# Exponentials and sines grouped by table set with two argument buffers in an SSM table, and one shared reciprocal for the attention denominators

## The chip, the cores and the metric

The kernel runs on one core of a Trainium2 chip. The metric is the device time of one execution in microseconds (us).

The engines are TensorE (PE in the profile, its weight loads PEld), VectorE (DVE), ScalarE (ACT), GpSimd (POOL) and SyncE (SP), which here only issues DMAs. Each engine works through its own stream of instructions.

## The reference, cut to what matters

Two independent computations share the input sizes and are written side by side in the output: linear attention with a softmax feature map (columns 0 to 447), and a diagonal state-space model as an FFT convolution (columns 448 to 895).

```python
# A: S = 2048, D = 448, 16 heads of 28
phi_q = concatenate([softmax(pq), softmax(-pq)], axis=-1)      # likewise phi_k
kv  = einsum("bhsf,bhsd->bhfd", phi_k, v)
z   = einsum("bhsf->bhf", phi_k)
num = einsum("bhqf,bhfd->bhqd", phi_q, kv)
den = einsum("bhqf,bhf->bhq", phi_q, z)[..., None] + 1e-6      # one value per head and row
o   = num / den
a   = o.transpose(...).reshape(B, S, D) @ wo

# B: D = 448 channels, N = 256 states, L = 2048
logdA = dt * (A_re + 1j * A_im);  dB = dt * (B_re + 1j * B_im)
P = exp(logdA[:, :, None] * l[None, None, :])
K = einsum("dn,dnl,dn->dl", C, P, dB).real                     # the table K
y = irfft(rfft(u) * rfft(K))[:L] + u * Dskip                   # per channel
```

## The kernel before: the parts that matter

The core works through four stages in turn: the attention; the coefficients of the SSM; the table K; the FFT convolution. The change touches the end of the attention and the table K.

*Attention denominators.* A denominator belongs to a head, not to each of its 28 columns. The kernel computed it for all columns: ZBBD holds the sums z repeated over each head's columns, and in each of 16 groups (4 column chunks dc, 4 row quarters sc) the denominators come out as a full tile, to be inverted in float32.

```python
for dc in range(4):
    for sc in range(4):
        # num_ps += KVBD.T @ PHIQ over 2 signs and 2 or 3 chunks   (L396)
        # den_ps += ZBBD.T @ PHIQ, as many matmuls again           (L408)
        nc.vector.tensor_scalar_add(den[plo:phi, :], dps[plo:phi, :], 1e-6)      # L417
        nc.vector.reciprocal(rden[plo:phi, :], den[plo:phi, :])                  # L419
        nc.vector.tensor_tensor(out=ot[...], in0=nps[...], in1=rden[...], op=ALU.mult)
```

*The table K.* A power exp(l·logdA) with l = 64·hi + lo is a product of a factor in hi (32 values) and one in lo (65 values). The factors in hi are built by a doubling recurrence on VectorE (UR, UI). Those in lo come from TensorE and ScalarE: a matmul of 4 rows makes their arguments (args), ScalarE takes Exp, cosine (Sin with a bias) and Sin of them, and VectorE multiplies. TensorE then contracts over the 128 states of a half. There are 2 halves of the states (nch) with 9 blocks of 48 slots and one of 16 each; a slot is one channel.

```python
for nch in range(2):
    # powers of the step, P[1] .. P[16] ("P tables"): VectorE
    for sb in range(0, NDQ, SBQ):                        # 10 blocks
        # 4 DMAs of coefblk; 10 small copies on GpSimd
        for k in (1, 2, 4, 8, 16):                       # recurrence: 6 VectorE operations a level, L628 to L633
            ...
        with tc.tile_pool(name=f"k_psarg{blk_idx}", bufs=1, space=PSUM) as psa_pool:
            for bq in range(0, nq, BQ):                  # 2 chunks of 24 slots
                args = psa_pool.tile([128, 8 * 512], F32, name="args", tag="args")    # 4096 columns; kps takes the same space
                for bs in range(nd):
                    nc.tensor.matmul(args[:, base:base + N_ARG], lhsT=coef[0:4, slot, :], rhs=R[0:4, :], ...)
                nc.scalar.activation(E[...],  argview(0),    ACT.Exp)                  # L661
                nc.scalar.activation(CL[...], argview(N_LO), ACT.Sin, bias=bias_hp)    # L662
                nc.scalar.activation(SL[...], argview(N_LO), ACT.Sin)                  # L664
                # WR = E * CL, WI = E * SL on VectorE
        with tc.tile_pool(name=f"k_psk{blk_idx}", bufs=1, space=PSUM) as psk_pool:
            # kps: 2 matmuls a slot of UR, UI with WR, WI; then to Ts by ScalarE (first half)
            # or added to Ts by VectorE (second half)
```

The softmax here doesn't subtract the row's maximum and nothing guards it: scores larger than these inputs give would overflow.

## Time and profile before

The median was 1204.45 us of 4 runs (1203.22 to 1206.53) when I predicted; with the runs made beside later ones, 1203.44 of 15. The stages of the profiled run, read from the first start of the instruction that opens each (dt is the first ScalarE operation of the coefficients, args the first matmul of K, the DMAs of the finished table close K):

| stretch | us |
|---|---|
| start to dt (attention) | 320.2 |
| dt to first args (coefficients) | 53.4 |
| first args to the table's DMAs (K) | 411.6 |
| the table's DMAs to the end (FFT) | 416.4 |

Three groups of the page of before say most. Each row has a line and what it does, then busy us and mean ns of one instruction, then the engine's idle time just before them and who ended it.

```profile
L644 PE MATMUL args<-Rconst,coefblk 4*128 4x130 bf16 x896 | 102.9, 308 | 169.6 <-ACT SL L664 126.6
...
L661 ACT ACT_TABLE_LOAD x39 | 50.0, 1283 | 77.8 <-PE args L644 74.6
...
L419 DVE RECIPROCAL rden_sb<-den_sb 128x512 f32<-128x512 f32 (+1 forms) x16 | 53.5, 3346 | 0.0
```

TensorE idles 126.6 us for ScalarE, and ScalarE 74.6 us for TensorE: the two wait for each other. The reciprocal has no idle time before it: there VectorE is the bound.

### The profile page before, as it was taken

How to read it: one execution, taken by the hardware profiler on the slowest of the kernel's cores; microseconds unless marked ns; L12 is line 12 of the kernel's file. 1: busy time of each engine (PE TensorE's matmuls, PEld its weight loads, DVE VectorE, ACT ScalarE, POOL GpSimd, SP SyncE). 2: the span in 40 equal slices, each digit the busy share in tenths (PEclk: the TensorE clock that was granted, in tenths of full speed). 3: DMA queues.
4: the chain of work that ended last, by engine and by line, in shares of the span. 5: the costliest groups of instructions: out<-in, count | busy, mean ns of one | idle time of the engine just before them, and what ended most of it. 6: DMA issues, size and time to landing. Idle time of an engine off the chain costs nothing.

```text
span 1201.6 us, 12236 instructions
## 1 busy us (share of the span) xinstructions
PE 544.9 (45%) x4427; PEld 243.1 (20%) x4427; DVE 639.1 (53%) x1301; ACT 401.4 (33%) x382; POOL 87.9 (7%) x243
## 2 busy tenths in 40 slices
PE   1986534867731333433243333311433345163198
PEld 0221100512111333333233323300100110010021
DVE  2339337569958865684766675439221223832500
ACT  0113320000016577667757576613221222031000
POOL 2000000100004321120211110010000000000000
PEclk9995665669575555555555555555555555555555
DMA  5000000000140000000000000051565557056511
GB/s 124 1 0 1 0 0 0 5 6 1 31 111 18 3 2 3 4 3 4 3 3 5 3 2 4 2 93 46 153 205 144 147 134 242 13 138 185 216 31 31
DMA packets 73636, 63.53 MB, mean 53 GB/s; under 512 B 34984, under 2 KB 68800, under 8 KB 73344
## 3 DMA queue, kind: packets, MB, share of 16 engines
q1 hardware_dynamic: 37866, 35.58, 11.2%
q10 hardware_dynamic: 35710, 27.17, 8.2%
q8 instruction: 35, 0.57, 0.2%
q14 instruction: 25, 0.20, 0.1%
HBM read 30.73 MB, written 28.52 MB: 49 GB/s over the span
## 4 chain that ended last, share of the span: by engine, by line
PE 28%; DVE 25%; DMA 20%; ACT 19%; issue 5%; ACTq 1%; SPq 1%; POOL 0%; DVEq 0%; POOLq 0%
PE args L644 7%; ACT CL L662 4%; DVE rden_sb L419 4%; ACT L662 4%; ACT SL L664 4%; PE ps_qk L195 3%; DMA SD_k<-stgA 3%; PE ops L1006 3%; PE ops L1004 3%; DVE stgA L882 2%; ACT L661 2%; DMA s2k<-SD_k 2%; DMA s2k<-SD_u 2%; DMA SD_u<-stgA 2%; DMA UD<-in_B_u_dram 2%
## 5 line engine op out<-in xcount | busy, mean ns | idle before, releaser
L644 PE MATMUL args<-Rconst,coefblk 4*128 4x130 bf16 x896 | 102.9, 308 | 169.6 <-ACT SL L664 126.6
L644 PEld LDWEIGHTS <-coefblk 4*128 4x128 bf16 x896 | 96.3, 142 | 173.7 <-issue 166.5
L871 PE MATMUL psA<-xin,FA 32*128 32x448 bf16 x128 | 52.1, 563 | 106.0 <-ACT stgA L880 33.4
L687 PE MATMUL kps<-WR,UR 128*32 128x65 bf16 x896 | 36.6, 256 | 127.8 <-ACT SL L664 115.9
L670 DVE TENSOR_TENSOR WR<-E,CL 128x1560 bf16<-128x1560 bf16 (+2 forms) x40 | 36.9, 922 | 105.4 <-ACT CL L662 105.4
L882 DVE CAST stgA<-psA 128x1792 bf16<-128x1792 f32 x16 | 32.4, 2024 | 82.8 <-DMA SD_k<-stgA 24.4
L661 ACT ACT_TABLE_LOAD x39 | 50.0, 1283 | 77.8 <-PE args L644 74.6
L661 ACT ACTIVATE E<-args 128x1560 bf16<-128x1560 f32 (+2 forms) x40 | 55.4, 1385 | 27.7 <-PE args L644 27.5
L439 ACT CAST osb<-ps_out 128x448 bf16<-128x448 f32 x8 | 4.2, 530 | 168.5 <-PE ps_out L430 158.4
L662 ACT ACTIVATE CL<-args,bias_hp 128x1560 bf16<-128x1560 f32 (+2 forms) x40 | 59.0, 1475 | 0.5
L880 ACT CAST stgA<-psA 128x1792 bf16<-128x1792 f32 x16 | 26.4, 1651 | 88.1 <-PE psA L871 28.6
L664 ACT ACTIVATE SL<-args 128x1560 bf16<-128x1560 f32 (+2 forms) x40 | 55.0, 1376 | 0.0
L689 PEld LDWEIGHTS <-UI 128*32 128x32 bf16 x896 | 32.7, 164 | 104.7 <-issue 101.7
L419 DVE RECIPROCAL rden_sb<-den_sb 128x512 f32<-128x512 f32 (+1 forms) x16 | 53.5, 3346 | 0.0
L195 PE MATMUL ps_qk<-xT,Wqkv 128*128 128x512 bf16 (+3 forms) x128 | 39.9, 425 | 28.7 <-DMA xT<-in_A_x_dram 26.6
L902 PE MATMUL xps<-s2k,CB 128*32 128x448 bf16 x256 | 31.6, 567 | 46.1 <-DMA s2k<-SD_u 22.9
L662 ACT ACT_TABLE_LOAD x40 | 51.3, 1283 | 0.2
L1004 PE MATMUL ops<-ZA,IA 128*32 128x448 bf16 x64 | 35.4, 556 | 35.3 <-DMA ZA<-ZD 35.3
L871 PEld LDWEIGHTS <-FA 32*128 32x128 bf16 x128 | 16.6, 131 | 140.9 <-issue 112.4
L969 PE MATMUL zps<-YF,IB 32*128 32x448 bf16 x64 | 23.2, 530 | 41.6 <-DVE YF L956 24.4
L672 DVE TENSOR_TENSOR WI<-E,SL 128x1560 bf16<-128x1560 bf16 (+2 forms) x40 | 36.5, 914 | 7.2 <-ACT SL L664 7.2
L687 PEld LDWEIGHTS <-UR 128*32 128x32 bf16 x896 | 33.6, 160 | 30.5 <-issue 15.1
(264 smaller groups left out, 1133.0 us busy)
## 6 DMA issues: line engine op xcount, KB each, us to landing
ZA<-ZD SPq DMA_DIRECT2D x1, 7168.0 KB
SD_u<-stgA SPq DMA_DIRECT2D x16, 224.0 KB
SD_u<-stgA ACTq DMA_DIRECT2D x16, 224.0 KB
s2k<-SD_u ACTq DMA_DIRECT2D x8, 448.0 KB
s2k<-SD_u SPq DMA_DIRECT2D x8, 448.0 KB
SD_k<-stgA SPq DMA_DIRECT2D x16, 224.0 KB
SD_k<-stgA ACTq DMA_DIRECT2D x16, 224.0 KB
s2k<-SD_k ACTq DMA_DIRECT2D x8, 448.0 KB
```

The costliest lines, as they stand in the source:

```text
L195: nc.tensor.matmul(ps[plo:phi, sc * 512:(sc + 1) * 512], lhsT=Wt[dci][dplo:dphi, fcol0:fcol0 + frows], rhs=xT[dci][dplo:dphi, sc * 512:(sc ...
L419: nc.vector.reciprocal(rden[plo:phi, :], den[plo:phi, :])
L644: nc.tensor.matmul(args[:, base:base + N_ARG], lhsT=coef[0:4, slot, :], rhs=R[0:4, :], start=True, stop=True)
L661: nc.scalar.activation(E[:, b0:b0 + nb, 0:ns, :], argview(0), ACT.Exp)
L662: nc.scalar.activation(CL[:, b0:b0 + nb, 0:ns, :], argview(N_LO), ACT.Sin, bias=bias_hp[:, :])
L664: nc.scalar.activation(SL[:, b0:b0 + nb, 0:ns, :], argview(N_LO), ACT.Sin)
L670: nc.vector.tensor_tensor(out=wr_v, in0=E[:, b0:b0 + nb, 0:ns, :], in1=CL[:, b0:b0 + nb, 0:ns, :], op=ALU.mult)
L672: nc.vector.tensor_tensor(out=wi_v, in0=E[:, b0:b0 + nb, 0:ns, :], in1=SL[:, b0:b0 + nb, 0:ns, :], op=ALU.mult)
L687: nc.tensor.matmul(outap, lhsT=UR[:, :, slot], rhs=WR[:, slot, :], start=True, stop=False, tile_position=(0, 32 * g))
L871: nc.tensor.matmul(ps[:, n2l * 512:n2l * 512 + D_MODEL], lhsT=FA2[0:32, :], rhs=xt[0:32, 4 * j + n2l, :], start=True, stop=True,)
L882: nc.vector.tensor_copy(stg[:, :, :], in_view)
L1004: nc.tensor.matmul(ops[32 * g2:32 * (g2 + 1), 0:D_MODEL], lhsT=IA[:, :], rhs=ZA[:, m2, :], start=True, stop=False, tile_position=(0, 32 * g2))
```

## The change

Its intent: to end the turn-taking in K, to halve the loads of activation tables, and to take the reciprocals out of the attention loop. The core of the diff, cuts marked with "...", first the attention:

```diff
-            t2 = bd_pool.tile([128, D_MODEL], BF16, name=f"ZBBD{fc}_{si}")
+            zi = bd_pool.tile([128, 32], BF16, name=f"ZIND{fc}_{si}")
...
-            nc.vector.tensor_scalar_mul(t2[:, :], HB[fc][:, :], zc[:, :])
+            nc.vector.tensor_scalar_mul(zi[:, 0:N_HEAD], IND[fc][:, :], zc[:, :])
...
+    for sc in range(4):
+        nc.gpsimd.dma_start(out=INDT4[32 * sc:32 * sc + N_HEAD, :], in_=INDT16[0:N_HEAD, :])
...
+        for sc in range(4):
+            idx = 0
+            for sgn in (+1, -1):
+                for fc in range(4):
+                    ci, fplo, fphi, fg0, fg1 = CHUNKS[fc]
+                    nc.tensor.matmul(
+                        dhp[32 * sc:32 * sc + 32, :],
+                        lhsT=ZIND[(fc, sgn)][fplo:fphi, :],
+                        rhs=PHIQ[(fc, sgn)][fplo:fphi, sc * 512:(sc + 1) * 512],
...
+        nc.vector.tensor_scalar_add(dtmp[:, :], dhp[:, :], 1e-6)
...
+            nc.vector.reciprocal(rdenh[:, :], dtmp[:, :])
...
-                nc.vector.tensor_scalar_add(den[plo:phi, :], dps[plo:phi, :], 1e-6)
...
-                nc.vector.reciprocal(rden[plo:phi, :], den[plo:phi, :])
...
+                    rbc[plo:phi, :],
+                    lhsT=INDT4[32 * sc:32 * sc + N_HEAD, g0:g0 + drows],
+                    rhs=rdenh[32 * sc:32 * sc + N_HEAD, :],
...
+                nc.scalar.copy(rbc_sb[plo:phi, :], rbc[plo:phi, :])
...
-                    in1=rden[plo:phi, :],
+                    in1=rbc_sb[plo:phi, :],
```

And in the table K, where the new code is, with its comments mine:

```diff
+         tc.tile_pool(name="k_psarg", bufs=2, space=bass.MemoryType.PSUM) as psa_pool, \
+         tc.tile_pool(name="k_psk", bufs=1, space=bass.MemoryType.PSUM) as psk_pool:
...
+        with tc.manual_schedule(engines={mybir.EngineType.PE}):      # TensorE in the program's order
...
+                    chunks = [(c0, min(18, nds - c0)) for c0 in range(0, nds, 18)]     # 18, 18, 12 slots
...
+                        args = psa_pool.tile([128, 3 * 512], F32, name="args", tag="args")
...
+                    for c0, nd in chunks:                            # all exponentials first
+                        args = arg_chunk(c0, nd, 0)                  # nd matmuls of 65 columns
+                        E = tabpool.tile([128, 3, 6, N_LO], BF16, name="E", tag="E", bufs=5)
...
+                            nc.scalar.activation(E[:, b0:b0 + nb, 0:ns, :], view(args, b0, nb, ns), ACT.Exp)
+                        Es.append(E)
+                    for (c0, nd), E in zip(chunks, Es):              # then all sines
+                        args = arg_chunk(c0, nd, N_LO)
...
+                            nc.scalar.activation(c, view(args, b0, nb, ns), ACT.Sin, bias=bias_hp[:, :])
+                            nc.scalar.activation(s, view(args, b0, nb, ns), ACT.Sin)
...
+                            nc.vector.tensor_tensor(out=w_r, in0=e, in1=c, op=ALU.mult)
+                            nc.vector.tensor_tensor(out=w_i, in0=e, in1=s, op=ALU.mult)
+                    if pending:
+                        emit_kmm(pending.pop(0))                     # kps matmuls of the block before
+                    pending.append((sb, nq, UR, UI, WR, WI, nch))
```

## The prediction

> **What bounds the kernel now.** I read the page's slices first, to see whether one engine is full; then the chain of waits, for its order in time; then stretches of time engine by engine; then the timeline of one repetition of each stage that the change touches.
>
> ```profile
> PE   1986534867731333433243333311433345163198
> DVE  2339337569958865684766675439221223832500
> ACT  0113320000016577667757576613221222031000
> PEclk9995665669575555555555555555555555555555
> ```
>
> No engine is full anywhere in slices 12 to 25 (about 360 to 780 us), and yet three are half busy: that is a stage whose engines take turns. It is the building of the table K (20 blocks: 2 halves of the state, each 9 blocks of 48 slots and one of 16). Just before it, VectorE shows 9 and 9: the attention denominators.
>
> ```profile
> core 0: us, PE busy (x) PEld busy (x) DVE busy (x) ACT busy (x) POOL busy (x), PEclk, DMA share, GB/s
> 462.19:483.26 21.07, 7.51 (x145) 7.09 (x144) 12.64 (x37) 14.94 (x12) 3.20 (x10) 0.50 0.01 3
> 625.29:646.45 21.16, 7.52 (x145) 7.09 (x145) 13.52 (x40) 13.92 (x10) 3.51 (x10) 0.50 0.02 4
> ...
> 373.58:785.20 411.62, 141.12 (x2688) 132.44 (x2688) 268.09 (x784) 279.38 (x223) 71.48 (x199) 0.50 0.01 3
> 253.00:320.00 67.00, 51.74 (x156) 15.47 (x154) 66.88 (x50) 0.53 (x1) 0.00 (x0) 0.81 0.01 4
> 320.00:373.58 53.58, 17.74 (x54) 5.00 (x54) 33.47 (x85) 8.00 (x17) 1.36 (x4) 0.63 0.32 86
> 785.20:1201.60 416.40, 180.58 (x643) 41.30 (x643) 151.09 (x168) 73.44 (x97) 4.67 (x8) 0.50 0.47 128
> ```
>
> The columns are: stretch, its length, busy time of each engine, clock, DMA. The first two rows are one block of the first and of the second half. A block takes 21.1 us though its fullest engine, ScalarE, works 14 to 15. In the denominators (253 to 320) VectorE works 66.88 of 67.00 us. The last row, the FFT convolution, is 416 us that the change does not touch.
>
> One block in the timeline (start, length, engine, what; in brackets the idle time before it and who ended it):
>
> ```profile
> 625.29 2.75 PE L644 MATMUL args<-Rconst,coefblk 4*128 4x130 bf16 x24 [0.75 <-DVE Ts L696]
> ...
> 628.11 1.28 ACT L661 ACT_TABLE_LOAD   x1 [5.64 <-PE args L644]
> ...
> 629.40 1.47 ACT L661 ACTIVATE E<-args 128x1560 bf16<-128x1560 f32 x1
> ...
> 630.88 1.28 ACT L662 ACT_TABLE_LOAD   x1
> ...
> 632.18 1.56 ACT L662 ACTIVATE CL<-args,bias_hp 128x1560 bf16<-128x1560 f32 x1
> ...
> 633.63 1.46 ACT L664 ACTIVATE SL<-args 128x1560 bf16<-128x1560 f32 x1
> ...
> 635.15 2.75 PE L644 MATMUL args<-Rconst,coefblk 4*128 4x130 bf16 x24 [7.11 <-ACT SL L664]
> ...
> 643.68 0.30 PE L687 MATMUL kps<-WR,UR 128*32 128x65 bf16 x4 [5.78 <-ACT SL L664]
> ```
>
> TensorE waits for ScalarE (7.11 us) and ScalarE for TensorE (5.64): args is one buffer of 4096 columns, so the next matmuls must wait until SL has read it, and the kps buffers take the same space. The block is the sum 2 x (args + loads + E, CL, SL) + kps. In the denominators one of 16 repetitions is:
>
> ```profile
> 261.99 3.34 DVE L419 RECIPROCAL rden_sb<-den_sb 128x512 f32<-128x512 f32 x1
> ...
> 265.25 0.63 DVE L417 TENSOR_SCALAR den_sb<-den_ps 128x512 f32<-128x512 f32 x1
> 265.79 0.67 DVE L420 TENSOR_TENSOR oT<-num_ps,rden_sb 128x512 bf16<-128x512 f32 x1
> ```
>
> The period is 4.39 us (261.99 to 266.38, where the next reciprocal starts), all VectorE.
>
> **What the Trainium skill says.** "ScalarE: Activation LUTs", section "Table sets: the hidden batching unit", advises doing all work of one table set before switching; its section "What ACT_TABLE_LOAD costs" gives about 2.7 us a load. The trace has loads before both E and CL, as the advice presumes, but of 1.28 us; I use the trace. Its 0.833 ns per element agrees: E takes 1471 ns at 1560 elements and 986 at 975, so 0.829 ns per element and 178 ns fixed. "VectorE: DVE Perf Modes", section "The perf-mode tier table", puts a bf16 tensor_tensor in SBUF at 2x (1224 ns for 2048); the WR products, 976 ns at 1560 and 678 at 975, give 0.509 ns per element and 181 fixed, which agrees. "TensorE: Matmul & The Clock Gate", section "Back-to-back issue gap", gives N / 1.2 GHz cold: 130 columns, 108 ns; here 24 matmuls take 2.75 us, 115 each, at the granted 0.50. "TensorEngine Tiling", section "Key Properties", says that a change of tiling mode drains TensorE: around 285 us, at full clock, three matmuls with one of 64 rows repeat every 0.855 us, three alike every 0.645, so 0.2 us a change.
>
> **The change part by part: the K stage.** It computes exponentials of all chunks first, sines after; chunks hold 18, 18 and 12 slots; args becomes two buffers of 1536 columns; kps gets its own 1024; the kps matmuls of a block are issued one block later, TensorE in program order.
> *ScalarE.* E for 1170, 1170 and 780 elements: 1.15 + 1.15 + 0.82 = 3.12 us. CL and SL start 1.46 us apart today, so each counts as E does: 2 x 3.1 = 6.2. Two loads in place of four: 2.57. Sum 11.9 us in the second half; in the first half plus two Ts copies of 0.51 (ScalarE's there): 12.9.
> *TensorE.* 96 matmuls of 65 columns in place of 48 of 130: the same columns, about 5.3 us, if the weight load hides behind 54 ns (estimate: the 128-column load takes 97 to 100 ns in isolation, no longer than a 32-column one, so yes). Kps 2 us. It fits under ScalarE: a chunk's args need about 1.3 us, and one sine chunk keeps ScalarE busy 2.3.
> *VectorE.* 12.64 and 13.52 us now. Six products in place of four: 2 x (0.78 + 0.78 + 0.58) = 4.26 us for 3.9, so 13.0 and 13.9. The recurrence (L608 to L633) is a chain on itself: it takes 10.0 us of wall for 8.75 busy, so up to 1.2 us more where nothing fills the gaps: 14.2 and 15.1.
> So the block is VectorE's after the change, not ScalarE's. I take values above the middle, 13.9 and 14.7 us, since each product also waits for its own ScalarE result. Nine of each: 257 us. Two small blocks at about 8 (30 short VectorE operations near 0.2 us, and products): 16. The P tables are VectorE's too and were hidden in ScalarE's turn until now: 11 us in the second half, 12 at the start. Drains of the delayed kps: 3. Sum 299; 412 - 299 = **113 us saved**.
>
> **The attention stage.** Removed: 80 denominator matmuls, 16 x (0.63 + 3.34) us of VectorE, HB (hidden before 226 us beside the kvps matmuls). Added, once: 32 matmuls for all heads' denominators, one addition (0.63) and one reciprocal (3.35) of 128x512; per repetition one 16-row matmul, a ScalarE copy (from L439: 0.53 us for 448 columns, so 0.58 for 512) and VectorE's product, 0.68. The indicator is now 16 columns wide.
> The last zcol casts run at 256.4 today, the DMAs behind them end about 255.5. Half the new denominator matmuls (positive sign) can run before; 16 more at 0.21 to 0.43 with drains take about 6 us, addition and reciprocal 4: about 266.5. Then TensorE bounds: 80 numerator and 16 broadcast matmuls at 0.215 (dense work before kept full clock from 281 to 315) are 20.6 us, plus about 50 mode changes of 0.2 us: 10; two groups are done early: about 29 us, so the last numerator ends near 296 in place of 319.7. The next work (coefficients, from ScalarE's dt at 320.2) starts when KVBD is released by that matmul, and then no longer waits 4 us for the last reciprocal. So 23.7 + 4 = 28: **28 us saved**. The 53 us from there to the first args hold DMA round trips and stay about 50.
>
> Sum: 113 + 28 = 141; 1204.45 - 141 = **1063 us**.
>
> **The rivals.** *ScalarE sets the block*, if VectorE's gaps are filled with products: 12.9 and 13.9. K then takes 9 x 26.8 + 42 = 283 us, total 1047. For it: ScalarE had the most busy time of any engine (279 of 412). *In-order VectorE stalls ScalarE*: a product queued behind the recurrence holds CL and SL (two buffers), and the exponentials of the next block could slip between sines, with two more loads (2.57 us). A block near 17 us gives 1063 + 18 x 2.7 = 1112. For it: VectorE's queue is in order and its slack is gone; against: the products were issued within the recurrence before (WR at 634.13). *TensorE stays cold in the attention loop*: 96 x 0.43 + 10 = 51 us, so 20 us of the 28 go: 1083. For it: the clock was 0.50 in most idle-ridden stretches; against: 0.81 in this one. *The gain is hidden*: if the DMA round trips and transposes of 320 to 373 did not wait for the attention, its 28 us would be lost, 1091. The timeline speaks against it: dt starts just after the last numerator.
>
> **Range and chances.** K between 280 and 330 and the attention saving between 12 and 36 give 1036 to 1098 if both go one way; I take 1030 to 1098 for 8 in 10. The removed turn-taking is over 100 us of a stage on the path, so a change under 2% (24 us) would need a broken schedule: faster 0.97, within 0.02, slower 0.01.
>
> **What would show it.** Right: K stage 280 to 320 us with VectorE over 85% busy; blocks of 14 to 15 us, longer in the second half; about 42 table loads in place of 79; no wait of args on SL beyond 1 us; 16 ScalarE copies in the attention, one 3.3 us reciprocal, first args near 341 us; 416 us from the K table's DMA to the end. Wrong: ScalarE or TensorE above 90% in K, more than 60 loads, first args after 360, or an FFT stage that changed.

## The result, and the profile after

The changed kernel is correct and takes 1055.06 us (median of 11 runs; the ten fast ones lie between 1049.48 and 1060.73), against 1203.44 for the kernel before. The ratio of the two is 0.8769, with a 95% interval from 0.8752 to 0.8787. This and the ratios below are the mean time of one kernel's fast runs over that of the other's in the same rounds, so not quite the ratio of the medians. Executions over 1.5% slower than the fastest of the same kernel are left out of the means. Predicted was 1063, with a range of 1030 to 1098.

The profiled run is the fastest of the changed kernel (1049.48 us). Its stages:

| stretch | before | after | predicted |
|---|---|---|---|
| start to dt | 320.2 | 294.4 | about 296 |
| dt to first args | 53.4 | 53.6 | about 50, the first args near 341 |
| K | 411.6 | 282.9 | 299 |
| FFT | 416.4 | 416.8 | 416 |

The busy slices of the page after, tenths in 40 slices of the span, as in the first block of the prediction:

```profile
DVE  1336804841463899999799993933322239330500
ACT  0013341000221589986887870412211120330000
PEclk9997555566995555555555555555555555555555
```

Slices 14 to 24 are K. VectorE now shows 9 in nearly all of them where no engine was above 8 before, and the two nines of the reciprocals are gone. The stretches of the changed kernel: end of the denominator matmuls, numerators, coefficients, K, FFT (length; busy time of PE, PEld, DVE, ACT, POOL with counts; clock; DMA share; GB/s):

```profile
253.00:261.34 8.34, 8.30 (x24) 1.88 (x23) 0.00 (x1) 0.00 (x0) 0.00 (x0) 0.72 0.00 0
261.34:293.00 31.66, 28.59 (x101) 8.86 (x100) 14.05 (x17) 8.87 (x16) 0.00 (x0) 0.95 0.00 1
293.00:348.05 55.05, 15.19 (x61) 5.13 (x60) 30.36 (x80) 9.16 (x19) 2.02 (x2) 0.71 0.32 86
348.05:630.90 282.85, 145.45 (x3584) 133.21 (x3584) 261.52 (x820) 231.66 (x239) 72.42 (x199) 0.50 0.02 5
630.90:1047.70 416.80, 179.82 (x643) 41.27 (x643) 151.09 (x168) 73.43 (x97) 4.67 (x8) 0.50 0.47 128
```

In K VectorE works 261.52 of 282.85 us, 92%; it worked 268 of 412 before. Its work has hardly changed; what vanished is its idle time. ScalarE is 82% busy. In the numerators it is TensorE that is nearly full (28.59 of 31.66), at a granted clock of 0.95. One block of the first half and one of the second, from one load of the Exp table to the next:

```profile
395.16:408.46 13.30, 6.14 (x167) 5.48 (x164) 12.36 (x39) 12.33 (x13) 3.16 (x10) 0.50 0.03 7
562.41:576.77 14.36, 7.72 (x192) 7.11 (x192) 13.42 (x41) 11.52 (x12) 3.20 (x10) 0.50 0.02 6
```

A block is VectorE's work plus 0.94 us in both halves. Within the second one the timeline reads (start, length, engine, what):

```profile
562.41 1.28 ACT L685 ACT_TABLE_LOAD   x1
...
563.70 2.90 ACT L685 ACTIVATE E<-args 128x1170 bf16<-128x1170 f32 x3
...
566.61 1.28 ACT L693 ACT_TABLE_LOAD   x1
...
567.91 1.24 ACT L693 ACTIVATE CL<-args,bias_hp 128x1170 bf16<-128x1170 f32 x1
...
570.23 0.81 PE L670 MATMUL args<-Rconst,coefblk 4*128 4x65 bf16 x12 [2.17 <-ACT SL L694]
```

There are two loads in a block where there were four, and the three exponentials follow each other without a gap: the next args are ready when ScalarE comes to them. TensorE still waits 2.17 us for SL, but it is ahead by a buffer and nobody waits for it. That wait must be read from the other side: over the whole run args wait 77.4 us for SL, yet ScalarE's exponentials wait only 1.4 us for args. ScalarE's largest wait in K is for VectorE: CL waits 36.7 us (16 times) for WR to free its buffer.

Of the attention, the denominator matmuls (start, length, what, in brackets the wait) show a thing to come back to:

```profile
251.97 0.61 PE L374 MATMUL dhp<-PHIQ_n,ZIND 64*32 64x512 bf16 x1 [0.72 <-DVE ZIND L360]
252.51 2.00 PE L374 MATMUL dhp<-PHIQ_p,ZIND 128*32 128x512 bf16 x4
254.44 2.00 PE L374 MATMUL dhp<-PHIQ_n,ZIND 128*32 128x512 bf16 x4
...
260.16 1.14 PE L374 MATMUL dhp<-PHIQ_n,ZIND 128*32 128x512 bf16 x4
```

The last ZIND operation of VectorE starts at 251.7. The matmul that waits for it is the first line, and 24 more of the 32 stand behind that one; the addition starts at 261.34. The single reciprocal takes 3.35 us.

### The profile page after: what moved, and what is told of

The parts are those of the page before. It is cut to its first block, busy times and chain, and to the rows that moved or that the text cites. A ratio compares the mean times of both kernels' runs of the same rounds, so it can differ in the third digit from the quotient of the medians.

```text
span 1047.7 us, 14006 instructions
## 1 busy us (share of the span) xinstructions
PE 524.5 (50%) x5291; PEld 238.1 (23%) x5291; DVE 571.5 (55%) x1288; ACT 363.2 (35%) x414; POOL 90.0 (9%) x250
## 4 chain that ended last, share of the span: by engine, by line
DVE 42%; DMA 24%; PE 23%; ACT 5%; issue 4%; ACTq 1%; SPq 0%; POOL 0%; DVEq 0%; POOLq 0%
PE ps_qk L195 3%; DVE WI L700 3%; DMA SD_k<-stgA 3%; PE ops L1013 3%; DVE WR L699 3%; PE ops L1011 3%; DVE UR L658 3%; DVE stgA L889 3%; DVE rt L656 3%; DVE rt L659 3%; DVE UI L661 3%; DMA s2k<-SD_k 2%; DMA s2k<-SD_u 2%; DMA SD_u<-stgA 2%; DVE rt L657 2%
## 5 line engine op out<-in xcount | busy, mean ns | idle before, releaser
L670 PE MATMUL args<-Rconst,coefblk 4*128 4x65 bf16 x1792 | 113.4, 238 | 159.4 <-ACT SL L694 77.4
L693 ACT ACTIVATE CL<-args,bias_hp 128x1170 bf16<-128x1170 f32 (+2 forms) x58 | 63.8, 1099 | 38.5 <-DVE WR L699 36.7
L694 ACT ACTIVATE SL<-args 128x1170 bf16<-128x1170 f32 (+2 forms) x58 | 58.4, 1008 | 1.7 <-DVE WI L700 1.7
L887 ACT CAST stgA<-psA 128x1792 bf16<-128x1792 f32 x16 | 26.4, 1651 | 86.7 <-PE psA L878 28.4
L685 ACT ACTIVATE E<-args 128x1170 bf16<-128x1170 f32 (+2 forms) x58 | 54.4, 1008 | 1.6 <-PE args L670 1.4
L1011 PE MATMUL ops<-ZA,IA 128*32 128x448 bf16 x64 | 35.4, 556 | 34.5 <-DMA ZA<-ZD 34.5
L417 ACT CAST rbc_sb<-rbc_ps 128x512 bf16<-128x512 f32 (+1 forms) x16 | 9.3, 585 | 121.0 <-PE rbc_ps L410 120.6
L699 DVE TENSOR_TENSOR WR<-E,CL 128x1170 bf16<-128x1170 bf16 (+2 forms) x58 | 39.3, 678 | 5.9 <-ACT CL L693 5.9
L700 DVE TENSOR_TENSOR WI<-E,SL 128x1170 bf16<-128x1170 bf16 (+2 forms) x58 | 39.0, 673 | 0.5 <-ACT SL L694 0.5
L988 DVE CAST Zs<-zps 128x448 bf16<-128x448 f32 x32 | 20.0, 625 | 33.6 <-PE zps L979 30.7
L986 ACT CAST Zs<-zps 128x448 bf16<-128x448 f32 x32 | 17.0, 532 | 59.8 <-PE zps L979 33.3
L1013 PE MATMUL ops<-UD,IDT 32*32 32x448 bf16 x64 | 34.7, 551 | 3.7 <-DVE UD L1003 3.7
```

What stands on the lines that cost most here:

```text
L670: nc.tensor.matmul(args[:, base:base + N_LO], lhsT=coef[0:4, c0 + bs, :], rhs=R[0:4, r0:r0 + N_LO], start=True, stop=True)
L685: nc.scalar.activation(E[:, b0:b0 + nb, 0:ns, :], view(args, b0, nb, ns), ACT.Exp)
L693: nc.scalar.activation(c, view(args, b0, nb, ns), ACT.Sin, bias=bias_hp[:, :])
L694: nc.scalar.activation(s, view(args, b0, nb, ns), ACT.Sin)
L699: nc.vector.tensor_tensor(out=w_r, in0=e, in1=c, op=ALU.mult)
L700: nc.vector.tensor_tensor(out=w_i, in0=e, in1=s, op=ALU.mult)
```

## The experiments

Twelve kernels ran. All times of before quoted with them are from the same rounds and the same chip. I give the length of the stages, since the total of one run also holds what varies in stages that the edit does not touch: over all these kernels dt starts between 294.4 and 299.4 us where the attention code is the same, and the FFT takes 416.3 to 421.2 us. So 10 us of a total, in one run, say nothing (the ten fast runs of the changed kernel alone spread over 11). The length of K is steadier: in the four kernels with the same code for it (the changed one, the second, ninth and eleventh) it is 282.8 to 283.2 us.

### Each part alone

The first kernel takes only the attention part of the change:

```diff
-def ssm_build_K(...):     # as changed
+def ssm_build_K(...):     # as in the kernel before
```

> The kernel before with the attention half of the change alone (denominators once for all heads); the K stage is that of before. Theory of the prediction, corrected by the trace after (last numerator 25.8 us earlier, first args 25.5 us earlier): 25 us less than before, so about 1178 us, K stage 411 us. Rival 'hidden': the transposes and round trips between the attention and the K stage take the gain, 1195 or more.

Measured: correct, 1184.54 us (4 runs, 1182.85 to 1187.42) beside 1203.64; ratio 0.985 (0.983 to 0.987). So the attention part is worth 19.1 us by the timed runs, where 25 were expected. In its profile dt starts at 296.1, 24.1 us earlier than before, the first args 23.4 us earlier, K takes 411.4, as before, and the FFT 421.2.

The second takes only K:

```diff
-(all of the file)         # as changed
+(all of the file)         # as in the kernel before, with ssm_build_K(...) as changed
```

> The kernel before with the K-stage half of the change alone. Theory (the two halves add): 129 us less than before, so about 1075 us, with a K stage of 283 us and VectorE busy over 90 per cent of it. Rival 'the halves interact': the K stage differs from 283 by over 6 us.

Measured: correct, 1075.56 us (4 runs, 1075.23 to 1078.89) beside 1203.64; ratio 0.895 (0.893 to 0.8971). K takes 283.2 us. So K is worth 128.1 us; with the 19.1 of the attention this makes 147.2, and the whole change gave 1203.44 - 1055.06 = 148.4. The parts add up: neither hides in the other.

### What in K carries the gain

The third kernel keeps all of the change except the grouping; each chunk's sines follow its exponentials:

```diff
     for c0, nd in chunks:
         args = arg_chunk(c0, nd, 0)
         ...                                   # E = Exp(args)
-        Es.append(E)
-    for (c0, nd), E in zip(chunks, Es):
         args = arg_chunk(c0, nd, N_LO)
```

> The kernel after, but each chunk's exponential stands next to its sines again: six table loads a block in place of two, both args buffers and the delayed kps stay. If the grouping matters, ScalarE becomes the bound: 9.3 us of activations + 6 x 1.28 us of loads = 17 us a block (18 in the first half), K stage about 345 us, total about 1117. Rival 'the second args buffer alone brings the gain and VectorE bounds anyway': blocks stay near 13.3 and 14.4 us, total within 10 us of 1055.

Measured: correct, 1107.7 us, one look. K takes 337.4 us, 54.5 more than with the grouping. The row of K:

```profile
351.20:688.60 337.40, 149.67 (x3584) 134.32 (x3584) 268.03 (x820) 326.67 (x309) 72.64 (x199) 0.50 0.02 4
```

ScalarE is now 97% busy (326.67 of 337.40) and bounds the stage, with six loads a block. The grouping is what moves the bound from ScalarE to VectorE.

The fourth takes the second args buffer away:

```diff
-tc.tile_pool(name="k_psarg", bufs=2, space=bass.MemoryType.PSUM)
+tc.tile_pool(name="k_psarg", bufs=1, space=bass.MemoryType.PSUM)
```

> The kernel after with one args buffer in place of two; grouped exponentials and delayed kps stay. If turn-taking was what cost, it comes back: six fills of 1.0 to 1.3 us (7.3 in all) beside 9.3 us of activations, loads hidden in the fills, about 16.6 us a block (17.6 in the first half), K stage about 340 us, total about 1112. Rival 'the table loads were the cost': blocks stay below 15 us, total below 1075.

Measured: correct, 1094.99 us, one look. K takes 323.6 us, 40.7 more, a second-half block 16.2 us. Its timeline shows the turns come back, on both sides:

```profile
574.77 1.15 PE L670 MATMUL args<-Rconst,coefblk 4*128 4x65 bf16 x18 [2.44 <-ACT SL L694]
```
```profile
575.96 1.24 ACT L693 ACTIVATE CL<-args,bias_hp 128x1170 bf16<-128x1170 f32 x1 [1.23 <-PE args L670]
```

TensorE waits for SL, then ScalarE for the args, and now that ScalarE waits it costs time. Both parts were needed: with the rest of the change in place, either one without the other leaves K at 324 to 337 us.

### Which engine bounds the changed K

If VectorE sets the block, less work for VectorE must shorten it and less work for ScalarE must not. Two kernels with a wrong result test that. The fifth replaces the last level of the recurrence by two copies:

```diff
 for k in (1, 2, 4, 8, 16):
+    if k == 16:
+        nc.vector.tensor_copy(UR[:, 16:32, 0:nds], UR[:, 0:16, 0:nds])
+        nc.vector.tensor_copy(UI[:, 16:32, 0:nds], UI[:, 0:16, 0:nds])
+        continue
```

> Level 16 of the recurrence (six VectorE products and sums per block) is replaced by two copies, so the result is wrong on purpose; VectorE loses about 2.6 us of work per block. Theory (VectorE sets the block in the changed kernel): the second-half block falls from 14.4 us to about 12, where ScalarE's 11.9 us take over, the first-half block from 13.3 to about 12.9 (ScalarE's sum there); K stage from 283 to about 255 us, total about 1025 to 1030. Rival (ScalarE or the args buffers set the block, VectorE only runs along): K stage stays within 5 us of 283, total about 1053.

The sixth drops SL:

```diff
 nc.scalar.activation(c, view(args, b0, nb, ns), ACT.Sin, bias=bias_hp[:, :])
-nc.scalar.activation(s, view(args, b0, nb, ns), ACT.Sin)
 nc.vector.tensor_tensor(out=w_r, in0=e, in1=c, op=ALU.mult)
-nc.vector.tensor_tensor(out=w_i, in0=e, in1=s, op=ALU.mult)
+nc.vector.tensor_tensor(out=w_i, in0=e, in1=c, op=ALU.mult)
```

> SL is dropped and WI is made from CL, so the result is wrong on purpose; ScalarE loses about 3.1 us per block and VectorE's work stays. Theory (VectorE sets the block): K stage stays between 271 and 283 us (VectorE was 92% busy, 261.5 of 282.9, and can't go below that), total about 1045 to 1055. Rival (ScalarE sets the block): 18 blocks lose up to 3.1 us each until VectorE's busy time stops it, K stage about 262, total about 1030.

Measured: 1016.67 and 1046.05 us, one look each, both wrong in the result as meant. The row of K in the lighter VectorE, then in the lighter ScalarE:

```profile
350.30:596.70 246.40, 145.34 (x3584) 133.31 (x3584) 219.46 (x740) 229.82 (x239) 64.93 (x199) 0.50 0.02 6
```
```profile
352.60:626.30 273.70, 145.19 (x3584) 133.43 (x3584) 259.01 (x820) 179.31 (x181) 79.10 (x199) 0.50 0.02 5
```

Taking 42 us of work from VectorE (261.5 to 219.5) shortened K by 36.5 us, more than the 28 expected; taking 52 us from ScalarE (231.7 to 179.3) shortened it by 9.2, hardly any of it in the regular blocks: they stay at 13.3 us in the first half and about 14.2 in the second. VectorE bounds the stage, as predicted, and in the lighter-VectorE kernel ScalarE has taken over (second-half block 11.5 us, of which ScalarE works 11.4). ScalarE was the very next bound: in the blocks shown above it works 1.9 us less than VectorE in the second half and as long in the first. So a first-half block gains only 1.0 us from the lighter VectorE (12.3 us), a second-half block 2.9.

### The delay and the program order

The seventh kernel issues a block's kps matmuls in their own block:

```diff
-if pending:
-    emit_kmm(pending.pop(0))
-pending.append((sb, nq, UR, UI, WR, WI, nch))
+emit_kmm((sb, nq, UR, UI, WR, WI, nch))
```

> The kps matmuls stand at the end of their own block instead of one block later, in the same program order on TensorE. Theory (the delay matters because TensorE is in order): the next block's args wait behind kps matmuls that wait for the block's last WI product, so ScalarE idles about 4.5 us a block (product 0.6, kps 2, args 1.2, queue), its period becomes about 16.5 us and the K stage about 330 us, total about 1100. Rival (VectorE's bound hides it, since the next recurrence runs meanwhile): K stage within 8 us of 283, total about 1055.

Measured: correct, 1070.86 us, one look; K 300.0 us. The direction was as my theory had it, the size not: 17.1 us where I expected 47. TensorE does stand in front of kps and wait for products, and the args queue behind it:

```profile
PE kps L610 <- DVE WR L699: 46.4, 22, 6.5
```

(46.4 us in 22 times, the longest 6.5.) But VectorE works on the next recurrence meanwhile, so that a block grows by only 0.9 to 1.0 us (14.28 and 15.28). What I left out is that this wait hides behind the engine that bounds.

The eighth lets the scheduler order TensorE's instructions:

```diff
-with tc.manual_schedule(engines={mybir.EngineType.PE}):
+if True:
```

> TensorE's instructions are ordered by the scheduler instead of by the program. Theory (program order is only a safeguard): the K stage stays within 8 us of 283 and the total within 1045 to 1065. Rival (the scheduler puts the kps matmuls of a block ahead of args that could run, so the turn-taking comes back): K stage 300 to 340, total 1070 to 1110.

Measured: correct, 1068.81 us, one look; K 296.9 us, 14 more. My theory (within 8 us) fell. In this order some kps matmuls stand between the args of one block. They wait for WR products, and the cosines behind them then wait for args (total us, times, longest):

```profile
PE kps L610 <- DVE WR L699: 95.3, 24, 9.0
...
ACT CL L693 <- PE args L670: 33.4, 13, 5.8
```

In the changed kernel these two waits are 5.5 and 1.6 us. So the program order on TensorE is a part of the gain, of 14 us, not a safeguard.

### Where 9 us of the coefficients went

From dt to the first args nothing was won though the coefficient loop itself got shorter: from dt to the last coefficient cast it took 27.0 us before and 20.8 after. From there to the first args it took 26.4 and then 32.9. In between lie twelve transposing DMA loads, issued alternately to the queues of SyncE and ScalarE. Three of the first six, after:

```profile
321.78 1.13 ACTq L509 DMA_TRANSPOSE tin_Bim<-in_B_B_im_dram  x1
...
324.24 1.12 SPq L509 DMA_TRANSPOSE tin_Bre<-in_B_B_re_dram  x1
...
326.73 1.13 ACTq L509 DMA_TRANSPOSE tin_Cim<-in_B_C_im_dram  x1
```

They start about 2.5 us apart, though each is 1.13 long. In the kernel before, the first three of the ScalarE queue ran one after the other:

```profile
347.94 1.15 ACTq L511 DMA_TRANSPOSE tin_Aim<-in_B_A_im_dram  x1
...
349.12 1.29 ACTq L511 DMA_TRANSPOSE tin_Bim<-in_B_B_im_dram  x1
...
350.45 1.27 ACTq L511 DMA_TRANSPOSE tin_Cim<-in_B_C_im_dram  x1
```

Among the twelve the queue changed three times before and seven times after, and from the first start to the last it took 18.1 and 24.5 us. The kernel with the attention part alone has the order of after, the one with K alone that of before; why the new attention leads to this order, no run shows. "DMA: Bandwidth & Descriptors" of the Trainium skill, section "Silent corruption: two transposing streams in flight at once", says that the transposes of one queue must wait for the full completion of those of another. That fits the trace, and it can be tested:

```diff
-eng = nc.sync if q_i % 2 == 0 else nc.scalar
+eng = nc.sync
 eng.dma_start(out=t[:, :], in_=src[:, nch * 128:(nch + 1) * 128], transpose=True)
```

> The twelve transposing loads of the coefficients all go to SyncE's queue instead of alternating with ScalarE's; nothing else differs from the changed kernel. Theory (the 6.5 us that the attention gain lost again between the last coefficient cast and the first args are the hand-over between two queues: 2.45 us from one transpose to the next when the queue changes, 1.2 us when it doesn't): the transposes follow each other about 1.2 us apart, and from dt to the first args it is about 47 us in place of 53.6. Rival (the transposes are slow for another reason, or something else ends later): dt to first args stays 52 to 55 us.

Measured: correct, 1048.47 us, one look. From dt to the first args it is 44.5 us, 9.1 less. The queue never changes now, and the twelve take 15.0 us from the first start to the last:

```profile
324.46 1.26 SPq L509 DMA_TRANSPOSE tin_Bim<-in_B_B_im_dram  x1
...
325.76 1.26 SPq L509 DMA_TRANSPOSE tin_Cre<-in_B_C_re_dram  x1
```

### A version that does less on the bounding engine

Since VectorE bounds K, and 18 of the 30 operations of a recurrence are so short (0.18 to 0.26 us for 48 to 192 elements) that most of each is a fixed cost (four times the elements take only 0.08 us more), the tenth kernel does the recurrence and the grouping for two blocks at once:

```diff
-SBQ = 12
+SBQ = 24                                   # 96 slots: 30 VectorE operations and 2 loads for twice the work
 # kps matmuls still for 12 of them at a time, one such part before the exponentials, one after the sines:
+if pending: emit_kmm(pending.pop(0))
 Es = []
 ...
-pending.append((sb, nq, UR, UI, WR, WI, nch))
+for qa in range(0, nq, 12):
+    pending.append((sb, qa, min(qa + 12, nq), UR, UI, WR, WI, nch))
 # buffers: E 5 -> 6, CL and SL 2 -> 3, rt1 and rt2 2 -> 1; and the transposes on one queue
```

> A candidate that should beat the changed kernel: the recurrence, the exponentials and the sines of two blocks (96 slots) are done together, so half the VectorE instructions of the recurrence and half the table loads; kps matmuls still per 48 slots and delayed; transposes on one queue. If VectorE sets the stage (as the light-VectorE run says), two blocks need VectorE 23.6 us in the first half and 25.4 in the second (recurrence 9.1 us of elements + 30 fixed costs of 0.18, products 8.5, copies 0.6, in the second half four additions of 0.45) in place of 26.6 and 28.7; ScalarE needs 23.4 and 21.3. K stage about 250 us, table loads about 25, total 1010 to 1030. Rival (products queue behind a recurrence that is now 14.5 us long, so ScalarE stalls and then bounds): 27 us or more for two blocks, K stage 270 or more, total 1040 or more.

Measured: correct, 1013.07 us (4 runs, 1010.24 to 1014.94) beside 1205.34; ratio 0.84 (0.8376 to 0.8424). The row of K:

```profile
349.10:593.20 244.10, 142.31 (x3584) 131.48 (x3584) 224.64 (x491) 201.29 (x216) 65.92 (x97) 0.51 0.02 5
```

VectorE has 37 us less to do in this row, with 329 instructions fewer, and K is 38.8 us shorter. A part of that only moved: some VectorE work of K (its first P tables) now runs before the first args, and from dt to the first args it takes 49.7 us, where the kernel with one queue takes 44.5. From dt to the table's DMAs, beside the kernel with one queue, the time is 33.5 us shorter (293.8 for 327.3) and VectorE's work 33.4 (258.17 for 291.62): the time follows the bounding engine's work one to one.

### Why the attention gave less than predicted

In the changed kernel 24 denominator matmuls stand behind the one that waits for the last ZIND. The loop runs over the quarter sc outside and over ZIND inside, so the first quarter needs all eight ZIND, and TensorE, in order, cannot begin the second quarter before. The eleventh kernel turns the loops around:

```diff
-for sc in range(4):
-    idx = 0
-    for sgn in (+1, -1):
-        for fc in range(4):
-            nc.tensor.matmul(dhp[32 * sc:32 * sc + 32, :], ...)
-            idx += 1
+for idx, (sgn, fc) in enumerate([(s_, f_) for s_ in (+1, -1) for f_ in range(4)]):
+    for sc in range(4):
+        nc.tensor.matmul(dhp[32 * sc:32 * sc + 32, :], ...)
```

> Only the order of the 32 denominator matmuls differs from the changed kernel: the four column quarters are the inner loop, so each matmul can run as soon as its own ZIND is there, and 4 instead of 24 are left after the last ZIND (TensorE is in order). Theory (the attention gained less than predicted because 24 of them, about 0.48 us each at the granted clock of 0.51, stood behind the last ZIND): the addition starts 2 to 3 us after the last ZIND instead of 10 to 12 us, at about 255 to 257 us, and dt starts near 288 to 291 in place of 294 to 299; total about 1045 to 1050. Rival (these matmuls keep TensorE warm for the numerators, which now run at half clock at first): the addition is earlier all the same, but dt starts at 294 or later.

Measured: correct, 1042.65 us, one look; dt starts at 287.1 us. The last four matmuls now take:

```profile
254.81 0.61 PE L372 MATMUL dhp<-PHIQ_n,ZIND 64*32 64x512 bf16 x4 [0.60 <-DVE ZIND L360]
```

The addition starts at 255.5, 1.0 us after the last ZIND operation (254.5), where it took 9.6 us in the changed kernel and 9.1 to 12.5 in the runs with the same attention code. The numerators do begin at half clock, as the rival said (0.43 us from one to the next until about 259), but nothing is lost by it: from the first of them to dt it is 30.9 us, against 32.3. I had not expected the four matmuls to take the time of one: each fills other 32 columns of the array, and "TensorEngine Tiling", section "Key Properties", says that different tiles can execute in parallel. In the old order four in a row shared a column strip and took 2.00 us at the same granted clock (0.50 and 0.51). (One of those four has 64 rows and the others 128; in the new order four of 128 rows take 0.62 us too.)

The twelfth kernel puts this order into the tenth:

> The wide blocks with one queue for the transposes, plus the new order of the denominator matmuls. If the two savings are on one chain they add: wide blocks gave 1013.1 us, the order takes 7 to 9 us more: 1003 to 1007 us, K stage 244 us unchanged. Rival (the numerators start cold, or the time before the first args ends elsewhere): 1010 to 1014.

Measured: correct, 1001.27 us (4 runs, 1000.54 to 1002.28) beside 1203.0; ratio 0.8322 (0.8295 to 0.835). K takes 244.1 us, dt starts at 287.1, and 48.7 us later come the first args. The two savings add, and this version beats both kernels: 54 us (5%) below the changed one.

## Why the prediction was right or wrong

**The total** was right: 1055 for 1063, inside the range. Two terms of the sum were off in opposite directions, K by 15 us and the attention by 9, so the closeness of the total is in part luck. The range was summed wrongly: K at 330 and an attention saving of 12 give 1204.45 - 82 - 12 = 1110, not 1098.

**What bounds K** was right. Turn-taking was the loss, VectorE the next bound at 92% busy (over 85% was asked for), blocks of the second half are longer, and the 42 table loads predicted for K are the 42 in its trace (82 in the whole run of before, 44 after). The two light kernels show VectorE as the bound by taking work away, and the two single-part kernels show that the grouping and the second buffer each carry a part (54 and 41 us).

**The size of K** was 15 us too small: 113 predicted, 128.7 in the profile, 128.1 in the kernel with K alone. The terms mis-sized are the block and the remainder. I took 13.9 and 14.7 us for a block, from VectorE's work of 13.0 and 13.9; measured are 13.3 and 14.4, with work of 12.36 and 13.42. The gaps, about 0.9 us, were as I sized them; the work was too long, because I added the lengths of single products (0.78 us), while in the trace the packed ones overlap: one WI starts at 562.42 and lasts 0.76, and the next WR starts at 563.10. Nine blocks of each half make 249 us in place of 257; what is left for small blocks, tables and drains is 283 - 249 = 34, where I had 42. Which of these terms holds the 8 us, the P tables, the small blocks or the drains, I did not separate.

**The sign "no wait of args on SL beyond 1 us"** was a bad one. The waits are 2 us and more, and harmless: TensorE is not the bound and runs a buffer ahead. The sign should have been ScalarE's waits for args, 1.4 us for the exponentials of the whole run.

**The attention** was predicted at 28 us: 23.7 to the last numerator and 4 for a reciprocal no longer waited for. By the timed runs of the kernel with it alone it gave 19.1; in that kernel's profile dt is 24.1 us earlier, as the first term says, and the first args 23.4. So in that profile the second term is missing, and the remaining 4.3 us were lost after the first args (the FFT, below). Two steps failed:

- "Half the new denominator matmuls (positive sign) can run before; 16 more ... take about 6 us." Only 7 ran before, the eighth waited for the last ZIND, and 24 followed; from the last ZIND operation to the addition it took 9.6 us in the profiled run of the changed kernel and up to 12.5 in others, at a clock of 0.5 to 0.7. The loop order shows why, and with the order turned dt started at 287.1. The profiles hid this miss, since I had put the last casts at 256.4 as in the kernel before and the last ZIND came at 251.7 in the changed kernel, the earliest of these runs (253.2 with the attention alone; the latest 256.4).
- "The 53 us from there to the first args ... stay about 50", with the first args near 341. The 4 us did come (in fact 6.2, in the coefficient loop), and the hand-over of the transposes between two queues took them back, 6.5 us. First args: 348.05. (The 341 does not follow from the prediction's own sum: 28 us before 373.6 is 345.6.) With one queue they go, and 2.6 us more.

One size in the sum was misread and did not show. "0.2 us a change" of tiling mode: three matmuls with one of 64 rows hold two changes, to 64 rows and back, so 0.855 - 0.645 = 0.21 us is for two, about 0.1 each. After the reciprocal the numerators still took the 29 us predicted (265.4 to 294.3), because eight output matmuls and some 3.4 us at half clock (0.43 us from one to the next between 267.8 and 271.2) fell into them; that is luck.

The rival "TensorE stays cold" was right for the denominators and wrong for the numerators, which ran at 0.95. What the prediction set against it was in part misread: in the kernel before, the granted clock was 1.00 from 281 to 303 us, but 0.50 from 304 to 315.

**The FFT stage** was to stay at 416 us. It was 416.8 in the profile of the changed kernel, but 421.2 in the one with the attention alone, and 416.3 to 421.0 in the others, with the same code; a part of the difference is the wait for the load of ZA (34.5 us in the changed kernel, 36.8 with the attention alone). The two kernels with the old attention show 416.4 and 416.9. Whether the new attention has a part in the longer ones, I did not settle; 4 to 5 us between the 23.4 seen at the first args and the 19.1 of the total depend on it.

**The rivals for K.** "ScalarE sets the block" put K at 283 us, which is the measured length to the microsecond, and still its mechanism was not what happened: without SL the blocks are hardly shorter (13.3 and about 14.2 us), with less VectorE work they are (12.3 and 11.5). Its number was met by luck: its pair of blocks, 26.8 us, was 0.9 too short and its remainder, 42, was 8 too long. "In-order VectorE stalls ScalarE" was there in kind (CL waits 36.7 us in all for WR), but not to 17 us a block, and K has only two loads beyond two a block.

## What to carry to other kernels

Where two engines take turns on one buffer and neither is full, sum up each engine's own work per repetition: the fullest one is the new time once the turns end, and here that gave the stage within 6%. Then ask what reaches the bounding engine late: on an in-order engine it is the loop order, not the dependency alone, that says how much is left after the last input comes. When the bound has moved, count the short instructions on the new bounding engine, for their fixed cost is the next thing to remove.

## What the Trainium skill lacked or had wrong

- "ScalarE: Activation LUTs", section "What ACT_TABLE_LOAD costs", puts a switch at 1283 ns for the load and 1380 ns for a drain. The trace has the 1283 ns and no room for the rest: the SL before it ends at 562.39, the load starts at 562.41, and the exponential follows at 563.70.
- "DMA: Bandwidth & Descriptors", section "Silent corruption: two transposing streams in flight at once", has the wait between queues but not its price: where the queue changes, the transposes here start about 2.5 us apart, on one queue about 1.3 us, and with seven changes among twelve the first args came 9.1 us later than with none.
